# Writing small products to four output quarters, and masking scores on VectorE instead of GpSimd

## The chip, the cores and the metric

The kernel runs on one core of a Trainium2 chip. The metric is the device time of one execution in microseconds. Three executions of the kernel before took 1001.75, 1011.66 and 1397.61 us, so the median is 1011.66; the last lies far off the other two. The engines are called as the profile calls them: PE is TensorE (PEld its weight loads), DVE is VectorE, ACT is ScalarE, POOL is GpSimd, SP is SyncE.

## The reference

A recurrent attention (RWKV-like) over 768 steps for 4 batches x 8 heads of width 40 feeds an MLP of 3072 tokens, width 320, hidden width 2048:

```python
for t in range(S):                       # S = 768; r, k, v, w, a, b are [4, 8, 768, 40]
    y[:, :, t] = einsum('bhd,bhde->bhe', r_t, state)
    Sa = einsum('bhde,bhe->bhd', state, a_t)
    state = state * w_t[:, :, None, :] - einsum('bhd,bhe->bhde', Sa, b_t)
    state = state + einsum('bhd,bhe->bhde', v_t, k_t)
x = y.transpose(0, 2, 1, 3).reshape(3072, 320)
h = x @ w_in                             # w_in [320, 2048]
g = where(h >= 1, h, where(h <= -1, 0, (h + 1)**2 / 4))
out = g @ w_out                          # w_out [2048, 320]
```

## The kernel before, in words

The 768 steps are cut into 24 chunks of 32 steps (`c`), and each chunk into two halves of 16 heads (`hb`). One (chunk, half) is a chain, so there are 48 chains. Within a chunk the recurrence becomes products of 32-row blocks: a unit triangular system is inverted per head, and the state (40x40 per head) is handed from chunk to chunk. Heads go in pairs `p` (0 to 7); the even head of a pair (`f` = 0) has its 40 feature rows at partitions 0 to 39, the odd one (`f` = 1) at 64 to 103. Their 32-row blocks of time steps lie crosswise in the other half of the partitions. A quarter is 32 partitions.

For each chain there are these steps, each with its line in the profile:

- `turn`: DVE transposes the loaded rows (L420, L423, L425).
- `scores`: 32 products of 40x32 by 40x32 (L435, L439) into one PSUM tile `ps`. Head `f` writes rows 64(1-f) to 64(1-f)+31, so two of the four output quarters are used, and the products of the two kinds alternate. ACT copies the two quarters into `cg` (L445), POOL multiplies them there by a strict triangular mask (L447).
- `chain`, five stages with a `yield` between. T1: 16 products with 64-wide stationary parts (L463), copied to `x0` by ACT (L468). T2, the second T product: 16 products over 32 rows (L473); head `f` reads and writes the same quarter `uq[f]`; DVE masks one part (L480), ACT negates the other (L484). Then the output and new state (L491; DVE L498, L503). Then the state transposition: 16 transposes, eight of `f` = 0 into one PSUM tile and eight of `f` = 1 into another, both at rows 0 to 39 (L520); ACT copies one to `ss` (L522), DVE the other (L523). Then the products with `ss` (L529; ACT L531).

`psum()` hands out four PSUM banks in turn; who gets a bank waits until its last reader is done.

Beside the chains, `moe` runs the MLP for finished groups of 64 time steps: L600 (into `ph`), ACT L606 and L607, DVE L613, ACT L587 (`gh`), POOL L588 (the remainder `gl`), and PE L574 with `gh` and L578 with `gl`. `background` runs the preparation of later superblocks of four chunks: `prelude` (rows; DVE L243, L252), `ab_set` (DVE L287, PE L298), and `invert` (POOL L326, L332; 31 pairs of operations per superblock, for five superblocks). L298 is a product of 40x32 by 40x32 whose 32 outputs go to all four quarters (`q = 2 * f + p % 2`), with `f` alternating.

The order is written out: the main loop calls `step` for the two chains of a chunk in turn; each `step` takes one stage of a chain and then three times feeds MLP work worth 1024 columns and background work up to its due share. Every engine then executes its own instructions in the order in which this program issued them, so an instruction that waits holds up all behind it on its engine. `scores` stands right before a state transposition in that order. An fp32 product appears in the trace as two instructions, a transpose as one: 32 scores products make 64 instructions, 16 transposes 16.

Of the kernel before, what the change touches and what calls it, by code (L numbers as in the profile page):

```python
# [15 lines left out]
ALU = mybir.AluOpType  # L16
# [3 lines left out]
NB, NHD, D, L = 4, 8, 40, 32  # L20
# [3 lines left out]
C_T, C_X, C_R, C_S, C_G, CW = 0, 32, 64, 96, 136, 176  # L24
# [3 lines left out]
    rows=[(0, 0), (20, 36), (38, 68), (68, 103), (107, 147)],  # L28
# [21 lines left out]
def rwkv_moe_kernel(ctx: ExitStack, tc: tile.TileContext, r, k, v, w, a, b, w_in, w_out, ident_d, mask_d, out):  # L50
    nc = tc.nc
# [10 lines left out]
    psum = lambda: psa.tile([128, 512], F32, tag="p2", name="p2", bufs=4)  # L62
# [5 lines left out]
    ident = const.tile([128, D], F32, name="ident")  # L68
    mask = const.tile([128, 32], F32, name="mask")
# [268 lines left out]
    def staged(key, needs, work_of):  # L338
# [14 lines left out]
        rows=("rows", None, prelude), ab=("ab", "rows", ab_set), inv=("inv", "ab", invert)).items()}  # L353
# [56 lines left out]

    evs = {}

    def turn(c, hb, part):
        u = 2 * c + hb
        cg, pr = cgs[u % 3], prs[u % 3]
        t5 = tis[c, hb].rearrange("p h (j x) -> p h j x", x=40)[:, :, :, 0:32]
        if part == 0:
            for f in range(2):
                rows = slice(64 * f, 64 * f + 64)
                nc.vector.transpose(cg[rows, f::2, C_X : C_X + 32], t5[rows, :, 4, :])  # L420
        elif part == 1:
            evs[u] = work.tile([128, 8, 2, 32], F32, tag="ev", name="ev")
            nc.vector.transpose(evs[u], t5[:, :, 1:3, :])  # L423
        else:
            nc.vector.transpose(pr[:, :, :, 8:40], t5[:, :, 0:4:3, :])  # L425

    def scores(c, hb):
        u = 2 * c + hb
        cg, pr, ev = cgs[u % 3], prs[u % 3], evs.pop(u)
        ps = psum().rearrange("p (h x) -> p h x", x=64)  # L430
        for p in range(8):
            for f in range(2):
                rows = slice(64 * f, 64 * f + D)
                q = slice(64 * (1 - f), 64 * (1 - f) + 32)
                nc.tensor.matmul(  # L435
                    ps[q, p, 0:32], lhsT=ev[rows, p, 1, :], rhs=cg[rows, 2 * p + f, C_X : C_X + 32],
                    start=True, stop=True,
                )
                nc.tensor.matmul(  # L439
                    ps[q, p, 32:64], lhsT=ev[rows, p, 0, :], rhs=pr[rows, p, 0, 8:40], start=True, stop=True  # L440
                )
        for f in range(2):
            q = slice(64 * (1 - f), 64 * (1 - f) + 32)
            o = cg[q, f::2, C_X : C_X + 64]
            nc.scalar.copy(o, ps[q])  # L445
            o = o.rearrange("p h (j x) -> p h j x", x=32)
            nc.gpsimd.tensor_mul(o, o, mask[q].unsqueeze(1).unsqueeze(1).broadcast_to([32, 8, 2, 32]))  # L447

    def chain(c, hb):

        u = 2 * c + hb
        cg, pr = cgs[u % 3], prs[u % 3]
        cgw = cgf[u % 3]
        cn, pn = cgs[(u + 2) % 3], prs[(u + 2) % 3]
        last = c == NC - 1
        uq = (slice(96, 128), slice(32, 64))
        er = [slice(64 * f, 64 * f + D) for f in range(2)]
        halves = (slice(0, 4), slice(4, 8))
        psv = psum_2()
        x0 = work.tile([128, 8, 72], F32, tag="x0", name="x0", bufs=1)  # L460
        for h in range(16):
            f = h % 2
            nc.tensor.matmul(  # L463
                psv[h // 8][64 * (1 - f) : 64 * (1 - f) + 64, h // 2 % 4, 0:72], lhsT=cg[:, h, C_T : C_T + 64],
                rhs=cg[:, h, C_R : C_R + 72], start=True, stop=True,
            )
            if h % 8 == 7:
                nc.scalar.copy(x0[:, halves[h // 8]], psv[h // 8][:, :, 0:72])  # L468
        yield
        psv = psum_2()  # L470
        for h in range(16):
            q = uq[h % 2]
            nc.tensor.matmul(  # L473
                psv[h // 8][q, h // 2 % 4, 0:72], lhsT=cg[q, h, C_T : C_T + 32], rhs=x0[q, h // 2, :],
                start=True, stop=True,
            )
        for i in range(2):
            for f in range(2):
                q = uq[f]
                nc.vector.scalar_tensor_tensor(  # L480
                    out=cg[q, f::2, C_R : C_R + 32][:, halves[i]], in0=psv[i][q, :, 0:32], scalar=-1.0,
                    in1=mask[q].unsqueeze(1).broadcast_to([32, 4, 32]), op0=ALU.mult, op1=ALU.mult,
                )
                nc.scalar.mul(cg[q, f::2, C_S : C_S + D][:, halves[1 - i]], psv[1 - i][q, :, 32:72], -1.0)  # L484
        yield
        psv = psum_2()
        n3 = 32 if last else 72
        yt = work.tile([128, 8, 32], F32, tag="yt", name="yt", bufs=1)
        for h in range(16):
            f = h % 2  # L490
            nc.tensor.matmul(  # L491
                psv[h // 8][64 * f : 64 * f + 64, h // 2 % 4, 0:n3],
                lhsT=cgw[:, h * CW + C_G : h * CW + C_G + 64], rhs=cg[:, h, C_R : C_R + n3], start=True, stop=True,
            )
        for i in range(2):
            if not last:
                for f in range(2):
                    nc.vector.scalar_tensor_tensor(  # L498
                        out=cn[er[f], f::2, C_S : C_S + D][:, halves[i]], in0=psv[i][er[f], :, 32:72], scalar=-1.0,
                        in1=pr[er[f], halves[i], 1, 39:40].broadcast_to([D, 4, D]), op0=ALU.mult, op1=ALU.mult,  # L500
                    )
        for i in range(2):
            nc.vector.tensor_tensor(  # L503
                out=yt[:, halves[i]], in0=psv[i][:, :, 0:32], in1=pr[:, halves[i], 1, 7:39], op=ALU.mult
            )
        yv = Y[0].rearrange("p a j b t -> p j b a t")[:, :, 2 * hb : 2 * hb + 2, :, 32 * (c % 2) : 32 * (c % 2) + 32]
        yt = yt.rearrange("p (b a) t -> p b a t", b=2)

        def round_y():
            nc.scalar.copy(yv[:, 0], yt)  # L510
            nc.gpsimd.tensor_sub(yv[:, 1], yt, yv[:, 0].bitcast(F32))

        yield
        if last:
            round_y()
            return
        pst = [psum()[:, 0:320].rearrange("p (h x) -> p h x", x=40) for _ in range(2)]
        for h in range(16):
            f, p = h // 8, h % 8
            nc.tensor.transpose(pst[f][0:D, p, :], cn[er[f], 2 * p + f, C_S : C_S + D], ident[er[f]])  # L520
        ss = work.tile([128, 8, 40], F32, tag="ss", name="ss", bufs=1)
        nc.scalar.copy(ss[0:D], pst[0][0:D])  # L522
        nc.vector.tensor_copy(ss[64 : 64 + D], pst[1][0:D])  # L523
        round_y()
        yield
        psv = psum()[:, 0:256].rearrange("p (h x) -> p h x", x=32)
        for h in range(16):
            f, p = h % 2, h // 2
            nc.tensor.matmul(psv[er[f], p, :], lhsT=ss[er[f], p, :], rhs=pn[er[f], p, 0, 8:40], start=True, stop=True)  # L529
        for f in range(2):  # L530
            nc.scalar.copy(cn[er[f], f::2, C_R : C_R + 32], psv[er[f]])  # L531
        yield
# [238 lines left out]
    i = 0  # L771
# [3 lines left out]
    def ahead(hb):  # L775
        for j in range(3):
            turn(0, hb, j)
        scores(0, hb)
        if NC > 1:
            load_ti(1, hb)  # L780
# [59 lines left out]
    for c in range(NC + 1):  # L840
        nxt = c + 1 < NC
        if c < NC:
            gens[c, 0] = chain(c, 0)
# [3 lines left out]
        if 0 < c < NC:  # L847
            scores(c, 1)
# [7 lines left out]
        if nxt:  # L856
            turn(c + 1, 0, 0)
        step(c, 0)
        if nxt:
            turn(c + 1, 0, 1)  # L860
# [4 lines left out]
        if nxt:  # L865
            turn(c + 1, 0, 2)
            if c + 2 < NC:
                load_ti(c + 2, 0)
        gens[c, 1] = chain(c, 1)
        if nxt:  # L870
            load_cg(c + 1, 1)
        step(c, 1)
        if nxt:
            scores(c + 1, 0)
# [44 lines left out]
```

## Time and profile before

| | |
|---|---|
| profiled execution | 1003.9 us, span 1002.1 us |
| busy: PE, PEld | 807.1 us (81%), 721.2 us (72%) |
| busy: DVE, ACT, POOL | 557.3, 530.9, 565.1 us |
| granted PE clock, mean | 0.854 of full speed |
| chain that ended last, by engine | PE 35%, POOL 19%, DMA 14%, DVE 14%, issue 7% |
| scores groups, from / to (T1 groups) | 48, first T1 at 79.3 us, last at 938.5 us |

Up to about 186 us the core prepares the first superblocks and converts weights, from there to 938.5 us chains and MLP run interleaved, and afterwards the rest of the MLP runs alone. "Busy" is the union of an engine's instructions; matmul ends are modelled, so in a series of small products what counts is the distance from the start of one group to the start of the next. In a row of the groups view stand count, total busy us and mean ns of one, and after the second bar the idle time before them with what ended it. In the waits view stand the waiting instruction, what released it, us in total, times, and the longest.

### The profile page before, as it was taken

Reading aid. Unit: us, or ns where it says so; the run is one execution under the profiler, and the core shown is the slowest. Engines: PE = TensorE matmul, PEld = TensorE weight load, DVE = VectorE, ACT = ScalarE, POOL = GpSimd, SP = SyncE. Lnnn points to the kernel's source line nnn. Section 1 sums busy time; section 2 is a strip of 40 time slices with the busy share of each in tenths; the row PEclk is TensorE's granted clock in tenths of the full one; section 3 lists DMA queues with packets and bytes.
Section 4 is the critical chain, followed back from the end, with each engine's and each line's share of the span. In section 5 each row is a group of like instructions: output and inputs, shape, how many; then the busy total and the mean of one; then the engine's idle time right before and its main releaser. Section 6 shows DMA issues by size and latency. Waiting matters only on the chain.

```text
span 1002.1 us, 34570 instructions
## 1 busy us (share of the span) xinstructions
PE 807.1 (81%) x14240; PEld 721.2 (72%) x14240; DVE 557.3 (56%) x1416; ACT 530.9 (53%) x1326; POOL 565.1 (56%) x769
## 2 busy tenths in 40 slices
PE   4523644476898888998888989888999899999995
PEld 3323643465787776887776978777898789999995
DVE  7873875764755655645735666734654344545221
ACT  5823554223654543555455555554675567667663
POOL 5220445787444897454897455996456974444432
PEclk9755555777998877889898898989998999999998
DMA  7798995653977845967465885655753535542010
GB/s 266 154 197 236 225 212 144 149 114 94 195 167 160 166 107 119 176 152 163 96 143 123 180 168 130 140 128 111 151 111 74 115 81 108 107 81 60 9 44 14
DMA packets 276862, 134.56 MB, mean 134 GB/s; under 512 B 194984, under 2 KB 266856, under 8 KB 276704
## 3 DMA queue, kind: packets, MB, share of 16 engines
q1 hardware_dynamic: 273504, 121.20, 56.4%
q0 software_dynamic: 3200, 11.14, 3.8%
q8 instruction: 112, 1.84, 0.9%
q14 instruction: 46, 0.38, 0.1%
HBM read 96.83 MB, written 33.82 MB: 130 GB/s over the span
## 4 chain that ended last, share of the span: by engine, by line
PE 35%; POOL 19%; DMA 14%; DVE 14%; issue 7%; SPq 6%; ACT 5%; POOLq 0%; DVEq 0%; ACTq 0%
PE ph L600 11%; PE po L574 5%; POOL lw L326 5%; POOL lw L332 5%; PE po L578 3%; DMA ti<-scr 3%; PE p L491 3%; POOL gl L588 3%; PE p L473 3%; PE p L463 3%; POOL cg L447 2%; DVE arena L243 2%; DMA ld_b<-in_b_dram 2%; PE p L435 2%; DVE rec L252 2%
## 5 line engine op out<-in xcount | busy, mean ns | idle before, releaser
L600 PE MATMUL ph<-X,w 120*128 120x256 f32 x1536 | 260.4, 307 | 22.9 <-DVE qt L613 18.9
L588 POOL TENSOR_TENSOR gl<-qt,gh 128x256 fp32r<-128x256 f32 x192 | 140.8, 733 | 227.6 <-ACT gh L587 212.0
L600 PEld LDWEIGHTS ph<-X,w 120*128 120x128 f32 x1536 | 220.3, 203 | 39.1 <-DVE qt L613 22.7
L613 DVE SCALAR_TENSOR_TENSOR qt<-qt,ph 128x256 f32<-128x256 f32 x192 | 79.9, 416 | 178.2 <-ACT qt L607 171.5
L574 PE MATMUL po<-wide,gh 128*128 128x320 f32 x768 | 163.0, 328 | 0.3 <-ACT gh L587 0.3
L587 ACT CAST gh<-qt 128x256 fp32r<-128x256 f32 x192 | 78.0, 406 | 159.2 <-DVE qt L613 158.5
L447 POOL TENSOR_TENSOR cg<-cg,mask 32x512 f32<-32x512 f32 x96 | 122.6, 1277 | 39.7 <-ACT cg L445 17.4
L578 PE MATMUL po<-wide,gl 128*128 128x320 f32 x384 | 101.5, 343 | 40.1 <-POOL gl L588 40.1
L606 ACT ACTIVATE qt<-ph,half_c 128x256 f32<-128x256 f32 x192 | 90.8, 473 | 73.4 <-POOL gl L588 65.7
L574 PEld LDWEIGHTS po<-wide,gh 128*128 128x128 f32 x768 | 123.9, 201 | 3.7 <-ACT gh L587 0.5
L326 POOL TENSOR_TENSOR lw<-lw 128x31 f32<-128x31 f32 (+15 forms) x155 | 93.8, 605 | 16.9 <-DMA lw<-abd 8.3
L578 PEld LDWEIGHTS po<-wide,gl 128*128 128x128 f32 x384 | 66.2, 199 | 48.4 <-POOL gl L588 45.9
L484 ACT ACTIVATE cg<-p 32x160 f32<-32x160 f32 x192 | 56.9, 296 | 78.1 <-DVE cg L480 47.6
L491 PE MATMUL p<-cg 128*64 128x72 f32 (+1 forms) x1536 | 72.3, 256 | 27.8 <-DVE cg L480 23.7
L491 PEld LDWEIGHTS p<-cg 128*64 128x64 f32 x1536 | 64.3, 161 | 37.5 <-ACT cg L484 28.6
L332 POOL TENSOR_TENSOR lw<-lw 128x31 f32<-128x31 f32 (+15 forms) x155 | 83.9, 541 | 8.8
L480 DVE SCALAR_TENSOR_TENSOR cg<-p,mask 32x128 f32<-32x128 f32 x192 | 55.7, 290 | 57.4 <-PE p L473 34.5
L607 ACT ACTIVATE qt<-qt 128x256 f32<-128x256 f32 x192 | 80.2, 418 | 6.1
L463 PE MATMUL p<-cg 128*64 128x72 f32 x1536 | 68.1, 247 | 18.0 <-DMA cg<-ttd 16.4
L463 PEld LDWEIGHTS p<-cg 128*64 128x64 f32 x1536 | 60.4, 153 | 25.2 <-issue 21.3
L498 DVE SCALAR_TENSOR_TENSOR cg<-p,pr 40x160 f32<-40x160 f32 x184 | 59.1, 321 | 34.7 <-PE p L491 32.8
L435 PE MATMUL p<-cg,ev 40*32 40x32 f32 x1536 | 63.1, 202 | 16.0 <-ACT x L468 7.2
(106 smaller groups left out, 1281.2 us busy)
## 6 DMA issues: line engine op xcount, KB each, us to landing
ti<-scr SPq DMA_DIRECT2D x96, 200.0 KB
ti<-scr SPq DMA_DIRECT2D x96, 168.0 KB
scr<-arena POOLq DMA_DIRECT2D x16, 640.0 KB, 5.7
cg<-scr SPq DMA_DIRECT2D x96, 80.0 KB
X<-Y SPq DMA_DIRECT2D x36, 160.0 KB
scr<-wide SPq DMA_DIRECT2D x8, 640.0 KB
tiab<-scr SPq DMA_DIRECT2D x32, 160.0 KB
scr<-in_r_dram SPq DMA_DIRECT2D x24, 160.0 KB
```

Source lines behind the costliest of these rows:

```text
L326: eng.tensor_mul(t3, W3[:, 0:n, j : j + 1].broadcast_to([128, n, m]), L3[:, j + 1 :, j].unsqueeze(1).broadcast_to([128, n, m]),)
L332: eng.tensor_sub(W3[:, 0:n, j + 1 :], W3[:, 0:n, j + 1 :], t3)
L435: nc.tensor.matmul(ps[q, p, 0:32], lhsT=ev[rows, p, 1, :], rhs=cg[rows, 2 * p + f, C_X : C_X + 32], start=True, stop=True,)
L447: nc.gpsimd.tensor_mul(o, o, mask[q].unsqueeze(1).unsqueeze(1).broadcast_to([32, 8, 2, 32]))
L463: nc.tensor.matmul(psv[h // 8][64 * (1 - f) : 64 * (1 - f) + 64, h // 2 % 4, 0:72], lhsT=cg[:, h, C_T : C_T + 64], rhs=cg[:, h, C_R : C_R ...
L491: nc.tensor.matmul(psv[h // 8][64 * f : 64 * f + 64, h // 2 % 4, 0:n3], lhsT=cgw[:, h * CW + C_G : h * CW + C_G + 64], rhs=cg[:, h, C_R : ...
L574: nc.tensor.matmul(pos[i], lhsT=gh[:, ts_], rhs=w2[f // 8][:, j, f % 8, :], start=f == 0 and j == 0, stop=False)
L578: nc.tensor.matmul(pos[i], lhsT=gl[:, ts_], rhs=w2[f // 8][:, 0, f % 8, :], start=False, stop=f == NF - 1)
L588: nc.gpsimd.tensor_sub(gl, gt, gh.bitcast(F32))
L600: nc.tensor.matmul(ph, lhsT=w1[:, wi, fs], rhs=Xs[g][:, xi, :], start=i == 0, stop=i == 7)
L606: nc.scalar.activation(gt, ph, AF.Relu, bias=half_c, scale=0.5)
L607: nc.scalar.activation(gt, gt, AF.Square)
```

## The change

Three groups of products write other PSUM rows, and the evictions move what they hold to the rows where it belongs.

- Scores: pair `p` writes quarter `f`, `p // 4` (rows 64(1-f) + 32 (p // 4)), so all four quarters are used, in half as many columns. The pairs go in the order 0, 4, 1, 5, 2, 6, 3, 7, with `f` alternating, first all 16 products of one kind, then all of the other. Four DVE operations of 32x256 multiply PSUM by the mask and write `cg`; ACT's copy and POOL's multiplication are gone.
- T2: the same quarters and order; its products alternate between two PSUM tiles. Evictions keep their engines and sizes.
- State transposition: instead of a transpose, an ordinary fp32 product with the identity as moving part and 64 stationary columns (40 of the state and 24 that follow it); `f` alternates, both halves go into one PSUM tile at rows 64f to 64f+63. ACT alone copies it to `ss`, all 128 rows.

```diff
+    quarter = lambda f, i: slice(64 * (1 - f) + 32 * i, 64 * (1 - f) + 32 * i + 32)
+    order = [4 * (n % 2) + n // 2 for n in range(8)]
...
     def scores(c, hb):
-        ps = psum().rearrange("p (h x) -> p h x", x=64)
-        for p in range(8):
-            for f in range(2):
-                rows = slice(64 * f, 64 * f + D)
-                q = slice(64 * (1 - f), 64 * (1 - f) + 32)
-                nc.tensor.matmul(
-                    ps[q, p, 0:32], lhsT=ev[rows, p, 1, :], rhs=cg[rows, 2 * p + f, C_X : C_X + 32],
-                    start=True, stop=True,
-                )
-                nc.tensor.matmul(
-                    ps[q, p, 32:64], lhsT=ev[rows, p, 0, :], rhs=pr[rows, p, 0, 8:40], start=True, stop=True
-                )
+        ps = psum()[:, 0:256].rearrange("p (h x) -> p h x", x=64)
+        for k in range(2):
+            for p in order:
+                for f in range(2):
+                    rows = slice(64 * f, 64 * f + D)
+                    nc.tensor.matmul(
+                        ps[quarter(f, p // 4), p % 4, 32 * k : 32 * k + 32],
+                        lhsT=ev[rows, p, 1 - k, :],
+                        rhs=pr[rows, p, 0, 8:40] if k else cg[rows, 2 * p + f, C_X : C_X + 32],
+                        start=True, stop=True,
+                    )
         for f in range(2):
             q = slice(64 * (1 - f), 64 * (1 - f) + 32)
-            o = cg[q, f::2, C_X : C_X + 64]
-            nc.scalar.copy(o, ps[q])
-            o = o.rearrange("p h (j x) -> p h j x", x=32)
-            nc.gpsimd.tensor_mul(o, o, mask[q].unsqueeze(1).unsqueeze(1).broadcast_to([32, 8, 2, 32]))
+            for i in range(2):
+                nc.vector.tensor_tensor(
+                    out=cg[q, f::2, C_X : C_X + 64][:, 4 * i : 4 * i + 4].rearrange("p h (j x) -> p h j x", x=32),
+                    in0=ps[quarter(f, i)].rearrange("p h (j x) -> p h j x", x=32),
+                    in1=mask[quarter(f, i)].unsqueeze(1).unsqueeze(1).broadcast_to([32, 4, 2, 32]),
+                    op=ALU.mult,
+                )
...
-        for h in range(16):
-            q = uq[h % 2]
-            nc.tensor.matmul(
-                psv[h // 8][q, h // 2 % 4, 0:72], lhsT=cg[q, h, C_T : C_T + 32], rhs=x0[q, h // 2, :],
-                start=True, stop=True,
-            )
+        for p in order:
+            for f in range(2):
+                q = uq[f]
+                nc.tensor.matmul(
+                    psv[p // 4][quarter(f, p // 4), p % 4, 0:72], lhsT=cg[q, 2 * p + f, C_T : C_T + 32],
+                    rhs=x0[q, p, :], start=True, stop=True,
+                )
...
-        pst = [psum()[:, 0:320].rearrange("p (h x) -> p h x", x=40) for _ in range(2)]
+        pst = psum()[:, 0:320].rearrange("p (h x) -> p h x", x=40)
         for h in range(16):
-            f, p = h // 8, h % 8
-            nc.tensor.transpose(pst[f][0:D, p, :], cn[er[f], 2 * p + f, C_S : C_S + D], ident[er[f]])
+            f, p = h % 2, h // 2
+            nc.tensor.matmul(
+                pst[64 * f : 64 * f + 64, p, :], lhsT=cn[er[f], h, C_S : C_S + 64], rhs=ident[er[f]], start=True, stop=True
+            )
         ss = work.tile([128, 8, 40], F32, tag="ss", name="ss", bufs=1)
-        nc.scalar.copy(ss[0:D], pst[0][0:D])
-        nc.vector.tensor_copy(ss[64 : 64 + D], pst[1][0:D])
+        nc.scalar.copy(ss, pst)
```

The changed file has other line numbers: scores products L438, masks L447, T2 L479 (DVE L486, ACT L490), transposition L526 (ACT L530), L529 becomes L536, and the MLP lines grow by 7.

On PE, around a late chain, from the end of the scores group to the MLP work behind T2; before (`p_...` are PSUM tiles, `ph`, `po_65`, `po_66` those of the MLP):

```order
L439 MATMUL p_12514<-pr_88,ev 32x32
L520 MATMUL p_12551<-ident,cg_85 40x40 x8
L520 MATMUL p_12552<-ident,cg_85 40x40 x8
L600 MATMUL ph_63<-X_1825,w_89 128x256 x4
L574 MATMUL po_65<-wide_916,gh 128x320 x2
L574 MATMUL po_66<-wide_916,gh 128x320 x2
L578 MATMUL po_65<-wide_916,gl 128x320
L578 MATMUL po_66<-wide_916,gl 128x320
L473 MATMUL p_12598<-x_12476,cg_84 32x72 x8
L473 MATMUL p_12599<-x_12476,cg_84 32x72 x8
L600 MATMUL ph_64<-X_1825,w_89 128x256 x8
```

The same place on PE after the change, from the start of the scores group:

```order
L438 MATMUL p_12436<-cg_85,ev 32x32 x16
L438 MATMUL p_12436<-pr_88,ev 32x32 x16
L526 MATMUL p_12473<-ident,cg_85 64x40 x16
L607 MATMUL ph_63<-X_1817,w_89 128x256 x4
L581 MATMUL po_65<-wide_916,gh 128x320 x2
L581 MATMUL po_66<-wide_916,gh 128x320 x2
L585 MATMUL po_65<-wide_916,gl 128x320
L585 MATMUL po_66<-wide_916,gl 128x320
L479 MATMUL p_12518<-x_12398,cg_84 32x72 x2
L479 MATMUL p_12519<-x_12398,cg_84 32x72 x2
```

The groups stand in the same order with the same MLP work between them; the transposition has one tile, and T2 alternates between two.

On DVE, the same chain before, from the last `turn` part to the MLP's L613:

```order
L425 STREAM_TRANSPOSE pr_88<-ti_81 128x16x32
L613 SCALAR_TENSOR_TENSOR qt<-qt,ph_64 128x256
L523 COPY ss<-p_12552 40x320
L420 STREAM_TRANSPOSE cg_83<-ti_80 64x8x32 x2
L480 SCALAR_TENSOR_TENSOR cg_84<-p_12598,mask 32x4x32 x2
L480 SCALAR_TENSOR_TENSOR cg_84<-p_12599,mask 32x4x32 x2
L613 SCALAR_TENSOR_TENSOR qt<-qt,ph_63 128x256
```

And after the change:

```order
L428 STREAM_TRANSPOSE pr_88<-ti_81 128x16x32
L620 SCALAR_TENSOR_TENSOR qt<-qt,ph_64 128x256
L447 TENSOR_TENSOR cg_85<-p_12436,mask 32x4x64 x4
L423 STREAM_TRANSPOSE cg_83<-ti_80 64x8x32 x2
L486 SCALAR_TENSOR_TENSOR cg_84<-p_12518,mask 32x4x32 x2
L486 SCALAR_TENSOR_TENSOR cg_84<-p_12519,mask 32x4x32 x2
L620 SCALAR_TENSOR_TENSOR qt<-qt,ph_63 128x256
```

The four masks stand where the copy of the transposed state stood.

On POOL, in a stretch with the inversion (`lw`), before:

```order
L326 TENSOR_TENSOR lw<-lw 128x207
L588 TENSOR_TENSOR gl<-qt,gh 128x256
L332 TENSOR_TENSOR lw<-lw 128x23x9
L326 TENSOR_TENSOR lw<-lw 128x192
L447 TENSOR_TENSOR cg_84<-cg_84,mask 32x8x64 x2
L511 TENSOR_TENSOR Y<-yt,Y 128x2x4x32
L332 TENSOR_TENSOR lw<-lw 128x24x8
```

And the same operations on POOL after the change:

```order
L326 TENSOR_TENSOR lw<-lw 128x207
L595 TENSOR_TENSOR gl<-qt,gh 128x256
L332 TENSOR_TENSOR lw<-lw 128x23x9
L326 TENSOR_TENSOR lw<-lw 128x192
L517 TENSOR_TENSOR Y<-yt,Y 128x2x4x32
L332 TENSOR_TENSOR lw<-lw 128x24x8
```

The two masks are gone from between the inversion's operations; nothing else moves.

More of the change, by code (lines that the diff above doesn't have):

```diff
@@ L480, in chain @@
                 nc.vector.scalar_tensor_tensor(
-                    out=cg[q, f::2, C_R : C_R + 32][:, halves[i]], in0=psv[i][q, :, 0:32], scalar=-1.0,
-                    in1=mask[q].unsqueeze(1).broadcast_to([32, 4, 32]), op0=ALU.mult, op1=ALU.mult,
+                    out=cg[q, f::2, C_R : C_R + 32][:, halves[i]], in0=psv[i][quarter(f, i), :, 0:32], scalar=-1.0,
+                    in1=mask[quarter(f, i)].unsqueeze(1).broadcast_to([32, 4, 32]), op0=ALU.mult, op1=ALU.mult,
                 )
-                nc.scalar.mul(cg[q, f::2, C_S : C_S + D][:, halves[1 - i]], psv[1 - i][q, :, 32:72], -1.0)
+                nc.scalar.mul(cg[q, f::2, C_S : C_S + D][:, halves[1 - i]], psv[1 - i][quarter(f, 1 - i), :, 32:72], -1.0)
         yield
```

## The prediction, on record before the result

> **What bounds the kernel now.** I read the page, then the busy time by stretch, then waits and groups, then the timeline of one undisturbed period. I cut the stretches where a T1 group (L463) starts: 48 chains, so 48 periods. Columns: window, length, then busy us of PE, PEld, DVE, ACT, POOL, granted clock, DMA share, GB/s.
>
> ```profile
> core 0: us, PE busy (x) PEld busy (x) DVE busy (x) ACT busy (x) POOL busy (x), PEclk, DMA share, GB/s
> 186.10:244.70 58.60, 37.49 (x515) 32.76 (x512) 31.33 (x80) 16.81 (x44) 47.97 (x71) 0.73 0.56 131
> 335.80:382.00 46.20, 38.13 (x530) 33.75 (x529) 23.46 (x49) 19.33 (x49) 43.06 (x61) 0.78 0.52 117
> 478.80:534.00 55.20, 47.36 (x793) 42.55 (x792) 28.46 (x67) 28.10 (x73) 50.98 (x74) 0.91 0.51 108
> 534.00:624.80 90.80, 84.11 (x1579) 75.03 (x1578) 61.04 (x169) 49.83 (x128) 46.41 (x64) 0.89 0.75 157
> 624.80:680.40 55.60, 46.89 (x793) 41.16 (x792) 29.33 (x68) 28.18 (x73) 51.68 (x74) 0.94 0.58 124
> 755.60:810.20 54.60, 47.78 (x795) 42.98 (x794) 19.53 (x51) 28.61 (x73) 48.31 (x72) 0.91 0.42 85
> 825.10:938.50 113.40, 113.40 (x2115) 103.45 (x2114) 54.29 (x146) 76.91 (x197) 49.59 (x57) 1.00 0.39 81
> ```
>
> The last row is 8 periods with PE busy throughout at full clock: 113.4 / 8 = 14.18 us each, the pace that PE alone would keep. The five short stretches (46 to 59 us) hold 2, 2, 3, 3 and 3 periods. There POOL is busy 82 to 93% and a period takes 18 to 29 us: the triangular inversion (L326, L332; a row below) is queued on POOL, and everything else on POOL stands in the same line. The other 29 periods between 244.7 and 938.5 are shorter on the whole; 534.0 to 624.8 is five of them. Before 186 us no expert MLP runs, and after 938.5 nearly only the MLP runs.
>
> What POOL's line costs, and who else is waited for:
>
> ```profile
> POOL gl L588 <- ACT gh L587: 212.0, 115, 7.5
> ACT qt L606 <- POOL gl L588: 65.7, 24, 6.6
> DVE ss L523 <- PE p L520: 53.6, 31, 4.2
> PE po L578 <- POOL gl L588: 40.1, 20, 6.2
> PE ph L600 <- DVE qt L613: 18.9, 14, 3.5
> POOL cg L447 <- ACT cg L445: 17.4, 19, 2.8
> PE p L529 <- DVE ss L523: 14.8, 4, 6.8
> ```
>
> PE waits longest, 40.1 us in 20 times, for POOL's gl (L588), the small remainder of an MLP tile. Its own operation takes 0.73 us; the rest is the line before it. The groups show what stands in that line.
>
> ```profile
> L588 POOL TENSOR_TENSOR gl<-qt,gh 128x256 fp32r<-128x256 f32 x192 | 140.8, 733 | 227.6 <-ACT gh L587 212.0 <-PE p L491 7.0 <-PE po L578 4.7
> L447 POOL TENSOR_TENSOR cg<-cg,mask 32x512 f32<-32x512 f32 x96 | 122.6, 1277 | 39.7 <-ACT cg L445 17.4 <-issue 13.4 <-PE p L520 1.8
> L326 POOL TENSOR_TENSOR lw<-lw 128x31 f32<-128x31 f32 (+15 forms) x155 | 93.8, 605 | 16.9 <-DMA lw<-abd 8.3
> L613 DVE SCALAR_TENSOR_TENSOR qt<-qt,ph 128x256 f32<-128x256 f32 x192 | 79.9, 416 | 178.2 <-ACT qt L607 171.5 <-POOL Y L511 2.1 <-POOL gl L588 1.4
> L480 DVE SCALAR_TENSOR_TENSOR cg<-p,mask 32x128 f32<-32x128 f32 x192 | 55.7, 290 | 57.4 <-PE p L473 34.5 <-ACT cg L484 20.8
> L445 ACT COPY cg<-p 32x512 f32<-32x512 f32 x96 | 55.4, 577 | 33.1 <-PE p L439 31.5
> L523 DVE COPY ss<-p 40x320 f32<-40x320 f32 x46 | 22.3, 484 | 54.2 <-PE p L520 53.6
> L522 ACT COPY ss<-p 40x320 f32<-40x320 f32 x46 | 18.9, 411 | 0.0
> ```
>
> **The change part by part.** *POOL.* Both masks of each scores group (L447) leave: 2 x 1.277 = 2.55 us per period. The view of L447 alone over the five POOL stretches sums to this:
>
> ```profile
> sum 270.20, POOL 33.07; mean POOL 6.61
> ```
>
> In those 270.2 us POOL sets the pace, so 33.1 us go. L447 also makes POOL stand still for ACT's copy, 17.4 us over all 96; the 26 in these stretches make 17.4 x 26 / 96 = 4.7 us. What is late next is PE, at 13 periods of under 14.2 us = 184 us, far below 270.2 - 37.8 = 232, so nothing new stops the gain. Term: -38. Bounds: a third of the mask time if DMA or DVE hold those periods anyway (-13); and, if PE's 40.1 us of waits all go and the clock is full, 270.2 - 40.1 - (217.7 busy now - 184) = 196, so -74. I stay near the mask's own time, since the inversion still fills POOL there.
>
> *ACT.* L445 goes, 2 x 0.577 us per period. ACT is busy 77 of 113 us in the undisturbed stretch; I cost this at nothing, in either direction. The ss copy (L522) still takes 320 columns, 0.41 us, now for both halves.
>
> *DVE.* Added: four masks of 32x256 out of PSUM. Nearest row is L613 with 256 columns at 416 ns: 1.66 us; bounds 4 x 290 (L480) and 4 x 484 (L523), 1.16 to 1.94. L523's 0.48 goes: net +1.18. In 31 of 46 periods DVE stood idle, 53.6 / 31 = 1.73 us on average, waiting for the transposition at exactly this place; the masks need only the scores, which end sooner, and fill that idle time. In the other 15 DVE is behind (rows stage) and 15 x 1.18 = 17.7 us are added ahead of L420, L480 and L613. ACT waits for L613, then POOL, then PE. PE waited for L613 or L523 18 times in 46 periods, so I put 0.39 of it on the path: +7, bounds 0 and +18.
>
> *PE.* The timeline of one undisturbed period, and three groups of other shapes and places (start, length, then the instructions):
>
> ```profile
> 842.09 0.26 PE L435 MATMUL p<-cg,ev 40*32 40x32 f32 x4
> ...
> 843.25 0.62 PE L520 MATMUL p<-ident,cg 40*40 40x40 f32 x16
> 843.80 0.74 PE L600 MATMUL ph<-X,w 120*128 120x256 f32 x4
> ...
> 845.35 1.19 PE L473 MATMUL p<-x,cg 32*32 32x72 f32 x32
> 846.47 1.22 PE L600 MATMUL ph<-X,w 120*128 120x256 f32 x8
> ...
> 848.20 0.80 PE L529 MATMUL p<-pr,ss 40*40 40x32 f32 x32
> 848.93 0.56 PE L578 MATMUL po<-wide,gl 128*128 128x320 f32 x2
> ```
> ```profile
> 265.70 0.76 PE L298 MATMUL p<-ea 40*32 40x32 f32 x64
> 266.38 0.85 PE L574 MATMUL po<-wide,gh 128*128 128x320 f32 x4
> ```
> ```profile
> 850.67 1.22 PE L491 MATMUL p<-cg 128*64 128x72 f32 x32
> 851.82 0.56 PE L574 MATMUL po<-wide,gh 128*128 128x320 f32 x2
> ```
> ```profile
> 947.10 1.12 PE L491 MATMUL p<-cg 128*64 128x32 f32 x32
> 948.15 0.56 PE L574 MATMUL po<-wide,gh 128*128 128x320 f32 x2
> ```
>
> What a group costs PE is the step to the next group's start. Scores (64 instructions, two output quarters) now take 843.25 - 842.09 = 1.16. L298 is the same shape and count, alternates the row halves, and already writes four quarters: 0.68. So scores: -0.48 (bounds 0 and -0.48). By the Trainium skill, "TensorE: Matmul & The Clock Gate", section "Wait — 56ns, not 53.3ns?", matmuls never start closer than about 25 ns, which would make the 64 take 1.6 us in either form. The L298 row disagrees: 0.68 / 64 = 10.6 ns.
>
> The second T product (L473) takes 1.12 for 32 instructions. No row shows it with four quarters; scaled as L298 to the scores, 1.12 x 0.68 / 1.16 = 0.66: -0.46 (bounds 0, and half, -0.56).
>
> The transposition (L520) takes 0.55 with 16 instructions. As an ordinary product each becomes two, as in L529 (16 products, 32 instructions), and its stationary part is 64 wide. Bounds: L529, 40 wide, 848.93 - 848.20 = 0.73; L491 with 72 moving columns, 851.82 - 850.67 = 1.15. L491's last chunk, 64 wide with 32 moving columns, is nearest: 948.15 - 947.10 = 1.05. So +0.50 (bounds +0.18 and +0.60). By the Trainium skill, same page, section "Terms", transpose mode is 4 times faster for FP32 than the ordinary product, which would make it 2.2 us. The L491 row speaks against that, though no run here shows this very product.
>
> Per period -0.48 - 0.46 + 0.50 = -0.44 (bounds -0.86 and +0.60), in the 29 periods where PE leads: -13 (bounds -25 and +17). In the POOL stretches it is hidden, and at the MLP's end nothing changes.
>
> *Waits.* T1 (L463) now needs the masks from DVE instead of POOL; it is the next T1 group, behind T, L529 (848.20) and an L491 group (850.67), so both are early. L529 needs ss from ACT alone, which has no L445 ahead of it. The transposition needs one PSUM buffer instead of two. All three cost nothing, and no queue of SP is touched.
>
> *Sum.* -38 + 7 - 13 = -44 against the profiled execution, 1003.9 us (span 1002.1 and 1.8 around it): 960. The median shown, 1011.66, lies 0.8% above that execution; I compare with 1003.9.
>
> **The rivals.** *POOL's line empties altogether.* The five stretches fall by 74: 1003.9 - 74 - 13 + 7 = 924. For it: PE's 40.1 us are all one wait. Against: the inversion's work stays where it is.
>
> *The masks leave POOL, but the stretches wait for something else.* The third: 1003.9 - 13 - 13 + 7 = 985. For it: PEclk 0.73 and 0.78 in the first two stretches and PE only 64% busy in the first. Against: POOL at 92, 93 and 88% in the later three.
>
> *Quarters don't overlap.* Scores and T product keep 1.16 and 1.12, the transposition pays +0.50: 29 x 0.50 = +15, so 1003.9 - 38 + 15 + 7 = 988. L298 speaks against it for the scores; T's 72 columns are open. The 25 ns rule named above would lead here.
>
> *The transposition at four times its time.* +1.65 - 0.94 = +0.71 per period, 29 x 0.71 = +21: 994. The "Terms" rule named above would lead here.
>
> *DVE becomes the bound (slower).* The four masks sit ahead of T's evictions and L613 in DVE's line. If DVE's idle time does not cover them, because a mask costs L523's 484 ns and the group before comes late, 42 x 1.94 = +81 replaces the +7: 1003.9 - 38 - 13 + 81 = 1034. It passes +20 us once more than (20 + 51) / 42 = 1.7 us per period is exposed, that is nearly all the masks. Against: DVE is busy 54 of 113 us in the undisturbed stretch and 61 of 91 in a busy one.
>
> **How the numbers follow.** Forecast 0.60; POOL empties 0.12; something else holds 0.09; no overlap 0.08; four times 0.04; DVE 0.07. 2% is about what a measurement of this kernel tells from no change, 20 us here. Faster: 0.60 + 0.12 = 0.72. Within: 0.09 + 0.08 + 0.04 = 0.21. Slower: 0.07. The range goes from the first rival, 924, past the 994 of the fourth to 998, where two of the bad bounds meet (POOL -13, PE +0 and DVE +7); outside lie the DVE rival and the worst pairs.
>
> **What would show it.** In the changed profile: L447's successor on DVE at about 0.42 us, four per scores group; no mask on POOL; the wait of PE for gl well under 40; the five stretches 6 to 9 us shorter each; an undisturbed period of 13.7 us; the scores group at 0.7, the T product at 0.66, the transposition at 1.05 to the next group's start. I am wrong if POOL stays over 90% busy in stretches that are no shorter, if T still takes 1.1, or if PE waits for L613's successor much over 19 us in all.

## The result, and the profile after

| | before | changed |
|---|---|---|
| median, us | 1009.42 | 976.55 (974.13 to 981.88) |
| ratio | | 0.971, 95% interval 0.963 to 0.978 |
| profiled execution: time, span, us | 1003.9, 1002.1 | 976.2, 974.4 |
| POOL busy, us | 565.1 | 443.8 |
| DVE busy, us | 557.3 | 590.4 |

The kernel before has a fourth execution here, 1007.18 us, which makes its median 1009.42. Ratios here and below leave out executions in a slow state, which lie more than 1.5% above the fastest of the same kernel: here the 1397.61 us, further on 997.92 us of one experiment and one of the kernel before, 1016.31 us.

The change is faster by 2.9%, inside the range (924 to 998) and on the side that was forecast; the forecast of 960 was 16 us too low. Busy time by stretch of the changed kernel, cut again where a T1 group starts (columns as in the prediction):

```profile
core 0: us, PE busy (x) PEld busy (x) DVE busy (x) ACT busy (x) POOL busy (x), PEclk, DMA share, GB/s
189.20:246.00 56.80, 35.42 (x549) 31.55 (x545) 33.23 (x86) 14.57 (x40) 42.99 (x67) 0.68 0.59 135
343.70:381.80 38.10, 32.62 (x561) 28.74 (x560) 24.18 (x55) 16.76 (x45) 35.74 (x53) 0.87 0.58 133
477.20:527.40 50.20, 44.70 (x843) 40.19 (x842) 30.48 (x77) 25.73 (x68) 43.88 (x69) 0.93 0.53 114
527.40:619.90 92.50, 82.11 (x1659) 73.06 (x1658) 61.01 (x184) 43.87 (x117) 33.16 (x52) 0.85 0.75 155
619.90:668.50 48.60, 44.32 (x843) 38.84 (x842) 32.36 (x77) 25.01 (x67) 44.43 (x68) 0.96 0.66 144
741.50:787.20 45.70, 43.18 (x841) 38.80 (x840) 23.12 (x60) 25.93 (x68) 41.24 (x67) 0.96 0.47 95
801.20:910.90 109.70, 109.70 (x2243) 99.87 (x2242) 63.79 (x170) 68.48 (x181) 29.66 (x41) 1.00 0.41 84
```

The five inversion stretches (the first three rows, the fifth and the sixth) take 239.4 us instead of 270.2: -30.8 (by stretch -1.8, -8.1, -5.0, -7.0 and -8.9). The eight undisturbed periods take 109.7 instead of 113.4, 13.71 each: -3.7. But the stretch of five periods with a superblock's rollover (where the rows of another superblock are loaded and prepared), 527.4 to 619.9, takes 92.5 instead of 90.8. All 29 periods between the stretches together: 482.3 after, 482.2 before. The start, up to the sixth T1 group, grew from 186.1 to 189.2, and the end is the same (63.5 and 63.6). So -30.8 + 0.1 + 3.1 - 0.1 = -27.7 us: the inversion stretches gained more than all of it.

PE's groups in an undisturbed period of the changed kernel (start, length):

```profile
804.01 0.46 PE L438 MATMUL p<-cg,ev 40*32 40x32 f32 x32
804.29 0.48 PE L438 MATMUL p<-pr,ev 40*32 40x32 f32 x32
804.70 1.13 PE L526 MATMUL p<-ident,cg 40*64 40x40 f32 x32
805.76 0.74 PE L607 MATMUL ph<-X,w 120*128 120x256 f32 x4
...
807.31 0.70 PE L479 MATMUL p<-x,cg 32*32 32x72 f32 x32
807.94 0.38 PE L607 MATMUL ph<-X,w 120*128 120x256 f32 x1
```

To the next group's start: scores 0.69, transposition 1.06, second T product 0.63. The masks on DVE in the groups view of the changed kernel, and then its view of who waits for whom:

```profile
L447 DVE TENSOR_TENSOR cg<-p,mask 32x256 f32<-32x256 f32 x192 | 80.6, 420 | 25.8 <-PE p L438 23.2
L595 POOL TENSOR_TENSOR gl<-qt,gh 128x256 fp32r<-128x256 f32 x192 | 140.9, 734 | 280.0 <-ACT gh L594 264.6 <-PE p L497 5.4 <-ACT cg L490 2.9
L607 PE MATMUL ph<-X,w 120*128 120x256 f32 x1536 | 260.9, 307 | 51.6 <-DVE qt L620 44.3 <-DMA X<-Y 6.5 <-issue 0.7
```
```profile
PE ph L607 <- DVE qt L620: 44.3, 14, 9.8
ACT qt L613 <- POOL gl L595: 39.7, 20, 7.1
DVE ea L287 <- DMA tiab<-scr: 18.4, 6, 6.0
PE po L585 <- POOL gl L595: 17.6, 12, 5.6
```

PE's wait for POOL's `gl` fell from 40.1 to 17.6 us. Its wait for DVE's MLP step (L620, before L613) rose from 18.9 to 44.3, 14 times in both; 10.6 us of that rise are in the first inversion stretch (4.5 to 15.1), the one that became only 1.8 us shorter. One of the longer waits of this second kind stands behind a transfer. The chain of waits of the changed kernel at one rollover, from 531 us:

```profile
531.21 5.84 DMA tiab<-scr
537.08 0.45 DVE ea L287
...
538.54 0.42 DVE cg L447
538.98 0.43 DVE cg L447
539.42 0.41 DVE cg L447
539.85 0.42 DVE cg L447
...
543.08 0.43 DVE qt L620
543.51 0.04 issue
543.55 0.80 PE ph L607 x2
```

DVE stood still until the rows of a new superblock (`tiab`) had landed. The masks stand behind that wait in DVE's line, so their 1.7 us came after the idle time and not into it, and PE got L620 only at 543.5. The same chain in the kernel before:

```profile
535.96 6.32 DMA tiab<-scr
542.30 0.45 DVE ea L287
...
542.86 1.20 DVE arena L243
...
545.01 0.48 DVE ss L523
...
548.33 0.43 DVE qt L613
548.81 0.79 PE ph L600 x2
```

From the landing to PE's `ph` it takes 6.5 us in both: the masks' 1.7 us took the place of the copy (0.48) and of a longer L243, which POOL's old masks held up (last section). What came later is the landing itself: 9.7 us after the T1 group at 527.4, before 8.3 us after that at 534.0.

### The profile page after: what moved, and what is told of

The parts are those of the page before. It is cut to its first block, busy times and chain, and to the rows that moved or that the text cites. A ratio compares the mean times of both kernels' runs of the same rounds, so it can differ in the third digit from the quotient of the medians.

```text
span 974.4 us, 35827 instructions
## 1 busy us (share of the span) xinstructions
PE 775.0 (80%) x14976; PEld 692.1 (71%) x14976; DVE 590.4 (61%) x1562; ACT 478.6 (49%) x1230; POOL 443.8 (46%) x673
## 4 chain that ended last, share of the span: by engine, by line
PE 34%; DMA 16%; POOL 16%; DVE 12%; issue 8%; SPq 8%; ACT 4%; POOLq 0%; ACTq 0%; DVEq 0%
PE ph L607 11%; PE po L581 6%; POOL lw L326 5%; POOL lw L332 4%; DMA ti<-scr 4%; PE po L585 3%; PE p L497 3%; POOL gl L595 3%; SPq L274 3%; PE p L468 3%; PE p L526 2%; DMA ld_a<-in_a_dram 2%; PE p L438 2%; PE p L479 2%; PE p L536 1%
## 5 line engine op out<-in xcount | busy, mean ns | idle before, releaser
L607 PE MATMUL ph<-X,w 120*128 120x256 f32 x1536 | 260.9, 307 | 51.6 <-DVE qt L620 44.3
L620 DVE SCALAR_TENSOR_TENSOR qt<-qt,ph 128x256 f32<-128x256 f32 x192 | 79.9, 416 | 150.3 <-ACT qt L614 148.3
L613 ACT ACTIVATE qt<-ph,half_c 128x256 f32<-128x256 f32 x192 | 91.1, 474 | 53.4 <-POOL gl L595 39.7
L585 PE MATMUL po<-wide,gl 128*128 128x320 f32 x384 | 99.6, 338 | 17.6 <-POOL gl L595 17.6
L497 PE MATMUL p<-cg 128*64 128x72 f32 (+1 forms) x1536 | 74.8, 262 | 44.2 <-DVE cg L486 39.7
L490 ACT ACTIVATE cg<-p 32x160 f32<-32x160 f32 x192 | 56.8, 296 | 87.9 <-DVE cg L486 61.0
L447 DVE TENSOR_TENSOR cg<-p,mask 32x256 f32<-32x256 f32 x192 | 80.6, 420 | 25.8 <-PE p L438 23.2
L486 DVE SCALAR_TENSOR_TENSOR cg<-p,mask 32x128 f32<-32x128 f32 x192 | 55.2, 288 | 36.2 <-PE p L479 30.7
L526 PE MATMUL p<-ident,cg 40*64 40x40 f32 x1472 | 57.1, 238 | 1.9 <-issue 1.9
```

The source lines that it names most:

```text
L447: nc.vector.tensor_tensor(out=cg[q, f::2, C_X : C_X + 64][:, 4 * i : 4 * i + 4].rearrange("p h (j x) -> p h j x", x=32), in0=ps[quarter(f, ...
L497: nc.tensor.matmul(psv[h // 8][64 * f : 64 * f + 64, h // 2 % 4, 0:n3], lhsT=cgw[:, h * CW + C_G : h * CW + C_G + 64], rhs=cg[:, h, C_R : ...
L585: nc.tensor.matmul(pos[i], lhsT=gl[:, ts_], rhs=w2[f // 8][:, 0, f % 8, :], start=False, stop=f == NF - 1)
L607: nc.tensor.matmul(ph, lhsT=w1[:, wi, fs], rhs=Xs[g][:, xi, :], start=i == 0, stop=i == 7)
L613: nc.scalar.activation(gt, ph, AF.Relu, bias=half_c, scale=0.5)
L620: nc.vector.scalar_tensor_tensor(out=gt, in0=gt, scalar=1.0, in1=ph, op0=ALU.min, op1=ALU.max)
```

## The experiments

Theory 1: the gain is POOL's line getting shorter. Theory 2: it is PE's shorter period. For the missing 16 us, theory 3: masks exposed on DVE; theory 4: at the rollovers transfers and SP's queue set the time, so what PE and DVE save there is not seen. Every time is given beside runs of the kernel before on the same chip; ratios are to that kernel, with their 95% interval, and 0.01 is 10 us.

**Only the masks moved.** The products stay in two quarters:

```diff
-            nc.scalar.copy(o, ps[q])
-            nc.gpsimd.tensor_mul(o, o, mask[q]...)
+            nc.vector.tensor_tensor(out=cg[q, f::2, C_X : C_X + 64], in0=ps[q], in1=mask[q]..., op=ALU.mult)
```

> The kernel before with one thing changed: the scores are masked by DVE straight out of PSUM (two operations of 32x512 per group), ACT's copy and POOL's masks are gone; all products stay as they were. If the gain of the whole change is POOL's line getting shorter (theory 1), most of it is here: POOL -31 us as seen in the five inversion stretches, DVE's extra work giving 10 to 20 back, so about 985 to 992 beside 1004. If the gain is PE's shorter period (theory 2, 13.73 instead of 14.18 us), nearly nothing of it is here: 1000 to 1008.

Measured 983.07 beside 1004.71, ratio 0.978 (0.974 to 0.981). Three quarters of the whole change's gain come from this alone, a little more than theory 1 expected and far from theory 2. The five inversion stretches take 244.4 us here, 25.9 less than before, and the undisturbed eight periods 113.4 as before.

**POOL's time given back.** POOL multiplies the masked scores by the mask once more, which leaves them as they are:

```diff
+            o = cg[q, f::2, C_X : C_X + 64].rearrange("p h (j x) -> p h j x", x=32)
+            nc.gpsimd.tensor_mul(o, o, mask[q].unsqueeze(1).unsqueeze(1).broadcast_to([32, 8, 2, 32]))
```

> The changed kernel, with POOL multiplying the masked scores by the mask once more (two operations of 32x512, as before the change), so that POOL's line is as long as it was and all else stays changed. Theory 1 (POOL's line): the gain of 28 to 30 us is gone, 1000 to 1008. Theory 2 (PE's period): at most a third is gone, 977 to 987.

Measured 1006.64 beside 1004.71, ratio 1.001 (0.998 to 1.004). The whole gain is gone. Its busy time by stretch:

```profile
189.50:248.10 58.60, 36.71 (x547) 32.46 (x545) 33.02 (x86) 14.54 (x40) 47.54 (x70) 0.68 0.54 131
344.20:389.50 45.30, 36.64 (x561) 31.73 (x561) 24.59 (x55) 17.07 (x46) 42.38 (x60) 0.79 0.55 123
484.70:541.20 56.50, 45.52 (x841) 40.78 (x840) 32.06 (x77) 25.19 (x67) 50.62 (x74) 0.88 0.49 105
630.60:688.10 57.50, 45.91 (x842) 40.49 (x842) 32.85 (x76) 25.00 (x67) 51.93 (x74) 0.94 0.60 126
761.50:815.90 54.40, 46.11 (x843) 41.28 (x842) 23.05 (x60) 25.38 (x67) 48.31 (x72) 0.91 0.41 87
830.30:940.00 109.70, 109.70 (x2241) 99.87 (x2240) 63.76 (x170) 68.48 (x181) 49.53 (x57) 1.00 0.41 83
```

The five stretches sum to 272.3, 32.9 more than in the changed kernel, and the masks' own time there was 33.0; POOL never stood idle for them there. The last row, the eight undisturbed periods, stays at 109.7: there POOL's time does not count. This shows theory 1, for the place and about for the size. POOL's masks also slow some operations of DVE (last section), but in these stretches L243 and L252 together took 43.0 us before and 40.6 after, too little for the gain.

**Masks done twice, and not at all.** The second kernel leaves the mask out of the result; ACT copies instead.

```diff
+        for _ in range(2):                      # masks twice: around the four multiplications
...
-                nc.vector.tensor_tensor(out=..., in0=ps[quarter(f, i)]..., in1=mask[...]..., op=ALU.mult)
+                nc.scalar.copy(cg[q, f::2, C_X : C_X + 64][:, 4 * i : 4 * i + 4], ps[quarter(f, i)])
```

> The changed kernel with DVE's four masks per scores group done twice (1.72 us more on DVE per period, POOL and PE as changed). If the missing 16 us of the forecast were lost to masks that stand in DVE's line behind transfers (theory 3), 0.4 or more of 46 x 1.72 = 79 us shows: 1005 to 1020. If they were lost because SP's queue and the transfers set the rollovers of a superblock whatever DVE does (theory 4), at most 10 us: 976 to 986.

> The changed kernel without the masks' multiplication: ACT copies the four quarters to their rows (four copies of 32x256), DVE has 1.72 us less per period, and the mask is left out of the result. Theory 3 (masks exposed on DVE): 0.4 of 79 us is won back, less a little for ACT: 945 to 962. Theory 4 (SP and transfers): 970 to 980.

Twice: 993.35, ratio 0.988 (0.984 to 0.992), some 17 us over the changed kernel's 0.971. That is 0.2 of the 81 us of work that were added to DVE, between what the two theories expected. In the undisturbed stretch eight periods took 113.2 instead of 109.7, so a second set of masks no longer fits DVE's idle time even there. Not at all: 973.68, ratio 0.970 (0.966 to 0.975), the changed kernel's ratio. Adding costs, taking away wins nothing: theory 3 does not explain the missing time, with the reserve that ACT had four copies more per group.

**The products one by one.** In the kernel before, only T2's quarters, then only the transposition as a product; in the changed kernel, the old transposition back. Their edits are the parts of the diff above.

> The kernel before with only the second T product writing four quarters, its evictions moved along; 0.63 instead of 1.12 us of PE per period. If PE's time counts in all 29 periods between the inversion stretches: -14 us, 990. If only the undisturbed ones gain, because the superblock rollovers wait for transfers (theory 4): -4 to -8, 996 to 1000.

> The kernel before with only the state transposition changed (ordinary product, 64 stationary columns, one PSUM tile, ACT alone copies it). PE pays 1.06 instead of 0.55 us per period, DVE loses a copy of 0.48. PE's time counted in 29 periods: +15, 1019. By theory 4 half of it: +7, and DVE's lighter line gives back up to 5: 1005 to 1011.

> The changed kernel with the old state transposition (transposes into two tiles, ACT and DVE copy one each). PE saves 0.50 us per period, DVE pays 0.48 more. PE's time counted in 29 periods: -15, 961; theory 4: -7 from PE and, at the 0.22 of added DVE time that the run with doubled masks showed, +5: 972 to 978.

T2 alone 1005.55 beside 1008.17, ratio 0.997 (0.994 to 1.000). The transposition alone 1012.61, ratio 1.006 (1.003 to 1.008). Old transposition in the changed kernel 973.43, ratio 0.967 (0.963 to 0.972), not told apart from 0.971. The sizes: 0.49 us less per period gained 3 us over the run, and 0.50 more cost 6, so a fifth to two fifths of what 29 periods would make. In the undisturbed eight periods the whole price shows: 113.4 became 109.4 with T2 alone and 117.4 with the transposition alone, and 109.7 became 106.4 with the old transposition back. Theory 2 falls, as does my step that PE's time counts in all 29.

**The layout transfers issued by POOL.**

```diff
 def relayout(g):
-            nc.sync.dma_start(
+            nc.gpsimd.dma_start(
```

> The changed kernel with the nine transfers that lay out a finished group for the MLP issued from POOL's queue instead of SP's. SP issues them back to back for 8.9 us ahead of the loads of a new superblock. Theory 4 (SP's queue delays the loads that DVE then waits for): 5 to 20 us faster, 956 to 971. If the transfers themselves take the time, or issuing them costs POOL as much: 974 to 990.

Measured 988.81 beside 1008.17, ratio 0.979 (0.973 to 0.985): slower than the changed kernel by some 8 us, with intervals that overlap. It could not tell whether SP's queue is the cause, since POOL paid for the issuing, as the groups view of this kernel shows:

```profile
L558 POOL DMA_DIRECT2D X<-Y x48 | 24.4, 514 | 0.0
L552 POOL DMA_DIRECT2D X<-Y x36 | 18.5, 521 | 1.2 <-POOL Y L517 1.2
L562 POOL DMA_DIRECT2D X<-Y x24 | 12.2, 513 | 2.9 <-PE p L497 2.3 <-DMA X<-Y 0.5
```

55 us came into POOL's line, and PE's wait for `gl` rose again, from 17.6 to 35.1. The inversion stretches take 264.7 us instead of 239.4, the 21 other periods before the undisturbed ones 362.5 instead of 372.6.

**Copies made twice.** A direct test of theory 4:

```diff
+        if s:
+            nc.sync.dma_start(twice4[s][c, :, :, o : o + D], x...[:, 4 * s + c])   # read by nobody
```

> The changed kernel with the 40 copies of r and v rows of superblocks 1 to 5 made a second time, to a place that nobody reads (6.4 MB and some 40 thousand packets more, 15% of all, and 40 x 0.65 us of SP's issuing). Theory 4 (the rollovers are set by transfers and SP's queue): 10 to 25 us slower, 986 to 1001. If DVE, POOL and PE set them: within 4 us, 972 to 980.

Measured 1003.76 beside 1007.61, ratio 0.996 (0.993 to 0.999): 26 us slower than the changed kernel, while the undisturbed periods take the same. Its busy time by stretch, the start, one inversion stretch and the undisturbed one:

```profile
0.00:197.30 197.30, 76.50 (x1758) 63.76 (x1759) 129.94 (x292) 82.40 (x184) 49.60 (x72) 0.61 0.86 196
638.30:699.80 61.50, 51.77 (x843) 45.80 (x842) 34.95 (x85) 26.59 (x71) 51.07 (x83) 0.81 0.69 135
830.30:939.90 109.60, 109.60 (x2241) 99.81 (x2240) 63.79 (x170) 68.34 (x181) 29.50 (x41) 1.00 0.41 84
```

The added copies cost time in several places. By place the profiled execution is 28.9 us longer: 8.1 in the start (197.3 us up to the sixth T1 group, 189.2 in the changed kernel), 14.1 in the inversion stretches, and only 6.8 in the 21 other periods, where the rollovers are. A single stretch is weak evidence: the second row is 61.5 instead of 48.6, but the kernel without the mask, which adds no transfer, takes 58.9 there. The run does not tell SP's issuing time from the transfers themselves, and it does not show that the rollovers wait for either.

**Three versions.** The transposition with 40 stationary columns, that with a later MLP start, and that with the copies of superblocks 2 to 5 moved into steps near the inversion stretches:

```diff
-                pst[64 * f : 64 * f + 64, p, :], lhsT=cn[er[f], h, C_S : C_S + 64], rhs=ident[er[f]], ...
+                pst[er[f], p, :], lhsT=cn[er[f], h, C_S : C_S + D], rhs=ident[er[f]], ...
...
-TRAIL = 5
+TRAIL = 6
...
+        s, i = now[0] // 40 + 1, now[0] % 40 - 10       # in step(); copy_rv leaves prelude()
+        if 2 <= s < NS and 0 <= i < 8:
+            copy_rv(s, i % 2, i // 2)
```

> The changed kernel with the state transposition's stationary part 40 columns wide instead of 64 (rows 40 to 63 of each half stay unwritten, so ACT copies ss in two operations of 40x320 instead of one of 128x320). If weight loading sets this group's pace, it takes what L529's group with 40 columns takes, 0.73 instead of 1.06 us, and the period is 13.4. Time: PE's 0.33 us counted in 29 periods -10, or by theory 4 about half, -5; ACT pays 0.41 more per period off the path: 966 to 972 beside 976.

> The kernel with the 40 column product, with the MLP starting one more step (3072 columns of work, some 2.8 us) behind the chains. Theory 4 says that leads counted in PE's work shrink when PE is faster: PE waited 4.7 us in three places for the group's layout transfers, each time followed by some us at half clock. Against the 40 column kernel alone: -3 to -8 if those waits were on the path, 0 to +3 (the later MLP tail) if not.

> The kernel with the 40 column product, and the copies of r and v rows of superblocks 2 to 5 moved out of the preparation of rows (where they stand at part starts) to eight steps of the main loop each, in and just before the inversion stretches, where transfers are fewer. Nothing else changes, the number of transfers stays. Theory 4 (transfers set the rollovers, as the doubled copies showed): 5 to 15 us faster than the 40 column kernel alone, 956 to 966. If it is the amount of transfers over the whole run and not their place: within 4 us of it, 967 to 975.

40 columns: 971.05 beside 1007.61, ratio 0.964 (0.961 to 0.967). The group took what was expected, 802.24 - 801.50 = 0.74 us, in PE's timeline:

```profile
801.50 0.81 PE L526 MATMUL p<-ident,cg 40*40 40x40 f32 x32
802.24 0.73 PE L608 MATMUL ph<-X,w 120*128 120x256 f32 x4
```

With the later MLP: 973.67, ratio 0.967 (0.964 to 0.970), no gain. With the copies moved: 965.59 beside 1006.33, ratio 0.960 (0.957 to 0.963), the lowest of all. Its six times, 959.68 to 969.97, all lie below the changed kernel's four, though those were taken beside other runs of the kernel before, and the intervals of the two ratios just touch. Against the 40 column kernel alone it is 0.4% lower with intervals that overlap. The gain stands where theory 4 puts it, 354.5 us instead of 365.2 in the 21 periods, but the kernel with the later MLP, its copies in place, takes 359.2 there; that the place of the copies matters is not shown.

## Why the prediction was right, and where it was off

- *The forecast's mechanism* (POOL's line) held and is shown by giving POOL its time back. The term was -38 and measured -30.8. What failed is the 4.7 us added for POOL waiting on ACT: I had shared the 17.4 us out evenly over all scores groups, but none of that wait lies in the five stretches (the view of L447 alone lists no idle time before it in any of them). That the rest agrees with the masks' own 33.1 us is in part luck. By stretch 1.8, 8.1, 5.0, 7.0 and 8.9 us went where 5.1, 5.1, 7.7, 7.7 and 7.6 of masks left; and of the kernels without masks on POOL (the one with layout transfers on POOL aside) the changed one has the shortest inversion stretches, 239.4 us beside 241.8 to 253.5. Those with masks on POOL take 265.5 to 276.0. Moving the masks alone gave 25.9; if the other 5 are not scatter, they came with the products, which I had called hidden there.
- *PE's group prices* held. Scores -0.48 forecast, -0.47 measured; T2 -0.46 and -0.49; transposition +0.50 and +0.51; period 13.73 and 13.71. The choice of L298 for four quarters and of L491's last chunk for a 64 wide stationary part were the right rows. The L298 row, and now the scores, 0.69 / 64 = 10.8 ns each, both disagree with the 25 ns of the Trainium skill's page "TensorE: Matmul & The Clock Gate", section "Wait — 56ns, not 53.3ns?". At equal width, 40 columns, the transposition as a product takes 0.74 instead of 0.55 us. The factor of 4 in that page's section "Terms" is not seen here either.
- *The term -13 for 29 periods failed*, together with DVE's +7: the 29 periods did not move (+0.1 instead of -6). The undisturbed eight gained the 3.7 us; the other 21 took 372.6 instead of 368.8. The step that was wrong is that PE leads in all periods outside the inversion stretches: in the undisturbed eight its price shows whole, in the other 21 not. At the rollover shown above PE waited for DVE, and DVE for transfers that landed 1.4 us later after the T1 group than before. That this is so at all rollovers is argued and not shown; the doubled copies lengthened these 21 periods by 6.8 us only.
- *The cover for the masks* holds in undisturbed periods only. There DVE's wait for the scores (23.2 us in all) took the place of the wait for the transposition (53.6), and the period is PE's own. I had priced the other 15 periods as DVE being behind with work; at 531 to 543 us it was DVE waiting for `tiab` with the masks queued behind, and there they made DVE's chain no longer than before.
- *A sign of being wrong came.* I had named a wait of PE for L613's successor much over 19 us; it was 44.3. In the first inversion stretch PE's wait for `gl` fell by 3.7 us, and this one rose by 10.6.
- *Left out:* POOL's masks leaving also made DVE's L243 and L252 shorter, by 11 us in the 21 other periods. DVE's busy time there grew by 12.7 us (227.7 to 240.4), where 21 times my +1.18 would be 25.
- *The start* was forecast unchanged and took 3.1 us more. Its cause is open: it varies from 184.8 to 191.9 us between the kernels here (197.3 with the copies doubled), and it is 188.8 with T2 changed alone.
- *The rivals.* The DVE rival did not come true, but the doubled masks show that it is near: 1.7 us more per period cost 17 us. The rival "the stretches wait for something else" was wrong for the inversion stretches as a whole, though in the first of them, where it pointed at PE being 64% busy, little was gained. Of the 29 periods between them, the 21 disturbed ones became no shorter, as that rival has it for the stretches. Neither product rival came true.

So 16 us were missing: 7 in the POOL term, 6 between the stretches, 3 at the start. Each is from one profiled execution of each kernel, and the 21 periods alone take 372.6, 377.1 and 365.2 us in the changed kernel and its versions with the old and the 40 column transposition, so the last two are hardly above scatter.

## What to carry to other kernels

Price work that is taken off an in-order engine by its own time in the stretches where that engine is the line others wait in; here 33 us in such stretches gave 26 to 33, while 123 us were removed in total. Do not share out a wait evenly over a count: look up in which stretches it lies. A saving on the engine with the highest busy share counts only in stretches where it waits for nothing, so split the span by what is waited for before multiplying by a count. When work moves to an engine with idle time, look at where in its queue it stands: in front of a wait it is covered, behind it it comes after the idle time. Then compare the whole chain before and after; here what the change took out of DVE's line made up for it.

## What was unexpected of the hardware

With the pairs ordered over four output quarters and both row halves, the second T product, with 72 moving columns, took 0.63 instead of 1.12 us, more than the scaling from the smaller shape gave (0.66). An ordinary fp32 product with the identity and 40 stationary columns costs 0.74 us for 16 heads, beside 0.55 for transposes and 1.06 with 64 columns. Issuing one layout transfer from POOL kept POOL busy for 0.51 us.

POOL's masks held up DVE. Before the change, the L243 of 1.20 us in the chain above ended at 544.06, when POOL's two masks had just ended (541.39 + 2.61 = 544.00):

```profile
541.39 2.61 POOL L447 TENSOR_TENSOR cg<-cg,mask 32x512 f32<-32x512 f32 x2
```

DVE's 112 operations of L252 took 53.6 us before and 43.2 after. The four kernels with masks on POOL need 449 to 482 ns for one, the ten without 356 to 400.
